# Two feed-forward layers behind an mLSTM: weights' low parts and one tile's high part of g move to GpSimd

## The chip, the cores and the metric

The kernel runs on one core of a Trainium2 chip. The metric is the device time of one launch in microseconds (us), the median of some runs. The core has five engines that run their own instruction streams in order and wait for each other through semaphores: TensorE (PE, with its weight loads as PEld), VectorE (DVE), ScalarE (ACT), GpSimd (POOL) and SyncE (SP), which here issues nearly all DMAs.

## The reference

```python
# per time step t, state C [D, D] and n [D] for each of 4 x 8 heads, D = 40, 768 steps
m_new = max(f_gate + m, i_gate)
f_stab, i_stab = exp(f_gate + m - m_new), exp(i_gate - m_new)
C = f_stab * C + i_stab * outer(v, k);  n = f_stab * n + i_stab * k
y = sigmoid(o_gate) * (C @ q) / max(abs(n . q), 1)
...
x = y, as [3072 tokens, 320]
x = relu(x @ w_in) ** 2 @ w_out            # layer 0: 320 -> 2048 -> 320
h = x @ w_in2                              # layer 1, the same sizes
out = where(h > 0, h, exp(min(h, 0)) - 1) @ w_out2
```

Everything is float32.

## The kernel before, in words

**Attention.** The recurrence is computed in chunks of 128 steps. One unit u is one chunk of one batch element (24 units), in two groups n = 2u, 2u + 1 of four heads. For a group, a row of stabilisers is loaded from DRAM, spread over 128 partitions (tile `mb`, L232), masked on GpSimd (L278), put through an exponential on ScalarE (four instructions at L286), and multiplied on VectorE with the scores from TensorE (L294, L300). `values` (L305, L310) makes a unit's outputs and state sums. VectorE adds them up (L333 to L342) and normalises (L349 to L353). GpSimd copies 64 columns of the result (L354). TensorE transposes it (L362, `in` from `xt`), and it becomes a part of the token tile x. GpSimd also multiplies the keys with a gate column (L274).

**Feed-forward.** Tokens go in six tiles of 512, and the 2048 inner columns in sixteen blocks m: 96 steps a layer. [...] A step is `mm1` (L468: eight matmuls with x's and the weights' high and low parts into the PSUM tile `h`), `elem` (the function, and the split of the result g into `hi` and `lo`), and `mm2` (L509: in layer 0 five matmuls with `hi`, then three with `lo`). In layer 0 `elem` is ReLU on ScalarE (L480), a square rounded to the high part `ghi` (L481), the same square in float32 in place (L482), and on VectorE `lo` = r - `hi` (L492). In layer 1 the high part is made by a GpSimd instruction (L491).

**Weights.** They come as 64-bit words (`raw`, L94) in 32 tiles of 704 columns, 16 a layer. ScalarE reads two fields of a word (L107, L108), VectorE puts a float32 together from them (L117, L118, L119: tile `ct`), ScalarE rounds the high part (`w_hi`, L127), and VectorE subtracts it from the whole for the low part (`w_lo`, L135). Layer 0's tiles are converted one a step, some five of them before the first step and the others during the first token tile; layer 1's during the last token tile of layer 0.

**Order.** Up to about unit 4 the order on TensorE, VectorE, ScalarE and GpSimd is that of the code. After that only TensorE's is; a scheduler places the others' instructions ahead of time, by its own estimates. TensorE writes `mm1` of step k + 1 ahead of `mm2` of step k, with a piece of attention between them in most steps. All DMAs stand in SyncE's one queue. Each engine executes its own list strictly in order.

Of the kernel before, what the change touches and what calls it, by code (L numbers as in the profile page):

```python
# [6 lines left out]
F32 = mybir.dt.float32  # L7
# [5 lines left out]
AF = mybir.ActivationFunctionType  # L13
ALU = mybir.AluOpType
# [26 lines left out]
def body(tc, qk, qp, kvo, gates, wq, ident_in, qkm_in, out):  # L41
    nc = tc.nc
    pe, act, dve, pool_, sp = nc.tensor, nc.scalar, nc.vector, nc.gpsimd, nc.sync
# [85 lines left out]
    def w_lo():  # L129
        if halves:  # L130
            i, t = halves.pop(0)
            l, f = ftiles[i]
            w = W[l, f]
            for a, k, o in [(640, 64, WC), (0, 640, WC + 64)] if l == 0 else [(0, WC, WC)]:
                dve.tensor_tensor(out=w[:, o:o + k], in0=t[:, a:a + k].bitcast(F32), in1=w[:, a:a + k].bitcast(F32), op=ALU.subtract)  # L135


    m_st = gc.tile([64, NCH + 1], F32, name="m_st")
# [333 lines left out]
    def elem(k):  # L472
        l, j, _, (c0, c1) = steps[k]
        n = c1 - c0
        h = HB.pop(k)[:, 0:n]
        r = gp.tile([128, TT], F32, tag="r", name="r")[:, 0:n]
        hi = gp.tile([128, TT], F32R, tag="ghi", name="ghi")[:, 0:n]
        lo = gp.tile([128, TT], F32R, tag="glo", name="glo")[:, 0:n]
        if l == 0:
            act.activation(out=r, in_=h, func=AF.Relu)  # L480
            act.activation(out=hi, in_=r, func=AF.Square)  # L481
            act.activation(out=r, in_=r, func=AF.Square)  # L482
        else:
            th = bp["t"].tile([128, TT], F32, tag="th", name="th")
            ex = bp["t"].tile([128, TT], F32, tag="ex", name="ex")
            act.activation(out=r, in_=h, func=AF.Relu, scale=-1.0)  # L486
            act.activation(out=th, in_=r, func=AF.Tanh, scale=0.5)  # L487
            act.activation(out=ex, in_=r, func=AF.Exp, scale=-1.0)  # L488
            dve.scalar_tensor_tensor(out=ex, in0=ex, scalar=1.0, in1=th, op0=ALU.add, op1=ALU.mult)  # L489
            dve.scalar_tensor_tensor(out=r, in0=h, scalar=0.0, in1=ex, op0=ALU.max, op1=ALU.subtract)  # L490
            pool_.tensor_scalar(out=hi, in0=r, scalar1=1.0, scalar2=1.0, op0=ALU.mult, op1=ALU.mult)  # L491
        dve.tensor_tensor(out=lo, in0=r, in1=hi.bitcast(F32), op=ALU.subtract)  # L492
        G[k] = (hi, lo)
# [174 lines left out]
    t = 2  # L668
    hs = lambda x, f: f(x) if 0 <= x < N0 else None
    us = lambda x, f: f(x // 2) if 0 <= x < N0 and x % 2 else None  # L670
    for i in range(N0 + 2):
# [19 lines left out]
        if i == N0:  # L691

            norm(B - 2)
            for f in trans(B - 2):
                f()
            x_hi(B - 2)
            idle(5)
            evac0(i - 1)
            norm(B - 1)
            x_lo(B - 2)  # L700
            for f in trans(B - 1, pacc.tile([128, 512], F32, tag="acc2", name="xt3")):
                f()
            x_hi(B - 1)
            x_lo(B - 1)
            idle(2)
            w_lo()
        if i == 0 or i > N0:
            w_begin(NF)
        if i == 2 or i > N0:
            w_lo()  # L710
# [6 lines left out]
        if i % 2 and i <= N0:  # L717
            if 1 < i < N0 - 1:
                w_lo()
            w_begin(NF)  # L720
# [24 lines left out]
    for k in range(-1, len(steps)):  # L745
        l, j, m, _ = steps[k] if k >= 0 else (0, 0, -1, None)
# [31 lines left out]
        for e in todo:  # L778
            elem(e)
# [77 lines left out]
```

## Time and profile before

| | |
|---|---|
| median of 3 runs | 869.37 us (866.83 to 874.54) |
| the profiled execution | 874.0 us, its span 870.3 us |
| granted TensorE clock, mean | 0.98 of full speed |
| TensorE matmuls busy | 824.0 us, 95% of the span |
| VectorE busy | 554.7 us, 64% |
| ScalarE busy | 540.1 us, 62% |
| GpSimd busy | 120.4 us, 14% |

The span goes from the first to the last instruction of the profiled execution. Shares over the whole span hide that the first 150 us and the rest have different limits, so the views below are by stretches. In a timeline a bracket behind an instruction says how long its engine stood idle before it and whose instruction ended that. The granted clock is TensorE's share of full speed, which falls to 0.5 in some stretches.

### The profile page before, as it was taken

What the parts mean: (1) busy time and instruction counts of PE and PEld (TensorE: products, weight loads), DVE (VectorE), ACT (ScalarE), POOL (GpSimd) and SP (SyncE); (2) the same over time, 40 slices, a digit from 0 to 9 for tenths busy, and PEclk for the clock granted to TensorE, in tenths of its full rate; (3) what the DMA queues carried; (4) which work ended last, traced back from release to release, by engine and by line L of the source; (5) the groups of instructions that cost most, each with busy time, mean ns of one, the idle gap of its engine ahead of it and who ended that gap; (6) DMA issues with size and microseconds to landing.
All of it is one profiled execution on the core that took longest, in us unless ns stands there. A gap on an engine that the chain in (4) does not pass through costs nothing.

```text
span 870.3 us, 14383 instructions
## 1 busy us (share of the span) xinstructions
PE 824.0 (95%) x5302; PEld 697.8 (80%) x5307; DVE 554.7 (64%) x994; ACT 540.1 (62%) x1035; POOL 120.4 (14%) x195
## 2 busy tenths in 40 slices
PE   9655988999999999999999998999999999999998
PEld 5544777788878878887888877999999999999997
DVE  6877995566555655645546987565565665655554
ACT  5767775665676766567558995464464554644543
POOL 3131111011111111010000002111111111111111
PEclk9978899999999999999999999999999999999999
DMA  8755563445453454445034550020020100000000
GB/s 272 227 171 180 191 197 93 134 139 141 129 143 105 128 155 119 138 129 142 2 124 142 191 171 23 1 78 1 1 79 1 49 31 2 31 1 1 31 1 31
DMA packets 32669, 85.39 MB, mean 98 GB/s; under 512 B 4087, under 2 KB 7895, under 8 KB 32599
## 3 DMA queue, kind: packets, MB, share of 16 engines
q1 hardware_dynamic: 32311, 84.15, 31.7%
q8 instruction: 41, 0.67, 0.3%
q10 hardware_dynamic: 288, 0.33, 0.1%
q14 instruction: 29, 0.24, 0.1%
HBM read 75.73 MB, written 8.73 MB: 97 GB/s over the span
## 4 chain that ended last, share of the span: by engine, by line
PE 76%; ACT 3%; DVE 3%; DMA 2%; issue 1%; POOL 1%; POOLq 0%; SPq 0%; ACTq 0%; DVEq 0%
PE h L468 35%; PE acc L509 35%; DMA mb<-negm_dr 2%; PE pv L305 1%; PE in L305 1%; PE s L294 1%; ACT mb L286 1%; PE in L362 1%; ACT ghi L481 1%; DMA kvo<-kvo 0%; DVE glo L492 0%; ACT r L480 0%; PE pv L310 0%; DVE r L490 0%; POOL mb L278 0%
## 5 line engine op out<-in xcount | busy, mean ns | idle before, releaser
L468 PE MATMUL h<-xh,w 128*128 128x512 f32 x1152 | 360.5, 394 | 0.2 <-ACT r L480 0.2
L468 PEld LDWEIGHTS h<-xh,w 128*128 128x128 f32 x1152 | 217.5, 189 | 45.3 <-ACT r L480 0.6
L492 DVE TENSOR_TENSOR glo<-r,ghi 128x512 fp32r<-128x512 f32 x192 | 133.5, 695 | 166.8 <-ACT r L482 86.1
L509 PE MATMUL acc<-w,ghi 128*128 128x320 f32 x768 | 170.3, 309 | 1.6 <-POOL ghi L491 1.6
L486 ACT ACTIVATE r<-h 128x512 f32<-128x512 f32 x96 | 57.5, 599 | 156.0 <-PE h L468 151.3
L468 PE MATMUL h<-xl,w 128*128 128x512 f32 x384 | 151.4, 394 | 0.0
L509 PEld LDWEIGHTS acc<-w,ghi 128*128 128x128 f32 x768 | 132.2, 188 | 9.8 <-POOL ghi L491 2.2
L509 PE MATMUL acc<-ghi,w 128*128 128x512 f32 x480 | 132.1, 403 | 7.3 <-ACT y L536 3.8
L509 PE MATMUL acc<-w,glo 128*128 128x320 f32 x384 | 119.1, 310 | 3.5 <-DVE glo L492 3.5
L491 POOL TENSOR_SCALAR ghi<-r 128x512 fp32r<-128x512 f32 x96 | 61.3, 638 | 361.7 <-DVE r L490 344.5
L509 PEld LDWEIGHTS acc<-ghi,w 128*128 128x128 f32 x480 | 88.2, 191 | 27.0 <-ACT y L536 6.6
L286 ACT ACTIVATE mb<-mb,cols 128x128 f32<-128x128 f32 x160 | 50.7, 389 | 81.0 <-POOL mb L278 81.0
L489 DVE SCALAR_TENSOR_TENSOR ex<-ex,th 128x512 f32<-128x512 f32 x96 | 66.5, 692 | 52.1 <-ACT ex L488 51.4
L509 PE MATMUL acc<-glo,w 128*128 128x512 f32 x288 | 84.1, 401 | 5.3 <-DVE glo L492 5.3
L468 PEld LDWEIGHTS h<-xl,w 128*128 128x128 f32 x384 | 72.8, 190 | 11.0
L480 ACT ACTIVATE r<-h 128x512 f32<-128x512 f32 x96 | 56.3, 587 | 33.7 <-PE h L468 33.1
L509 PEld LDWEIGHTS acc<-w,glo 128*128 128x128 f32 x384 | 72.1, 188 | 4.6 <-DVE glo L492 4.6
L509 PEld LDWEIGHTS acc<-glo,w 128*128 128x128 f32 x288 | 55.2, 193 | 18.8 <-DVE glo L492 6.9
L278 POOL TENSOR_SCALAR_AFFINE_SELECT mb<-mb 128x512 f32<-128x512 f32 x40 | 29.5, 748 | 281.7 <-DMA mb<-negm_dr 206.6
L481 ACT ACTIVATE ghi<-r 128x512 fp32r<-128x512 f32 x96 | 60.2, 627 | 13.3 <-PE acc L509 12.9
L490 DVE SCALAR_TENSOR_TENSOR r<-h,ex 128x512 f32<-128x512 f32 x96 | 66.3, 691 | 3.0
L487 ACT ACTIVATE th<-r 128x512 f32<-128x512 f32 x96 | 60.8, 633 | 2.7
(100 smaller groups left out, 892.3 us busy)
## 6 DMA issues: line engine op xcount, KB each, us to landing
raw<-wq SPq DMA_DIRECT2D x32, 704.0 KB, 4.3
rqk<-qk SPq DMA_DIRECT2D x32, 480.0 KB, 4.3
kvo<-kvo SPq DMA_DIRECT2D x24, 488.0 KB, 4.8
mb<-negm_dr SPq DMA_DIRECT2D x40, 256.0 KB, 4.6
qp<-qp SPq DMA_DIRECT2D x20, 256.0 KB, 4.0
y_dr<-y SPq DMA_DIRECT2D x18, 256.0 KB, 2.4
out<-y SPq DMA_DIRECT2D x22, 160.0 KB, 1.8
yr<-y_dr SPq DMA_DIRECT2D x12, 256.0 KB, 2.6
```

The source lines that it names most:

```text
L278: pool_.affine_select(out=m, in_=m, pattern=[[0, 4], [1, L]], compare_op=ALU.is_ge, fill=NEG, base=0, channel_multiplier=-1)
L286: act.activation(out=m[:, i, :], in_=m[:, i, :], func=AF.Exp, bias=cols[c % 2][:, col:col + 1])
L468: lambda i=i, a=a, b_=b_: pe.matmul(h[:, 0:n], lhsT=a, rhs=b_, start=(i == 0), stop=(i == len(seq) - 1))
L480: act.activation(out=r, in_=h, func=AF.Relu)
L481: act.activation(out=hi, in_=r, func=AF.Square)
L486: act.activation(out=r, in_=h, func=AF.Relu, scale=-1.0)
L487: act.activation(out=th, in_=r, func=AF.Tanh, scale=0.5)
L489: dve.scalar_tensor_tensor(out=ex, in0=ex, scalar=1.0, in1=th, op0=ALU.add, op1=ALU.mult)
L490: dve.scalar_tensor_tensor(out=r, in0=h, scalar=0.0, in1=ex, op0=ALU.max, op1=ALU.subtract)
L491: pool_.tensor_scalar(out=hi, in0=r, scalar1=1.0, scalar2=1.0, op0=ALU.mult, op1=ALU.mult)
L492: dve.tensor_tensor(out=lo, in0=r, in1=hi.bitcast(F32), op=ALU.subtract)
L509: ops.append(lambda: pe.matmul(o, lhsT=l_, rhs=r_, start=first and st, stop=last and sp_))
```

## The change

The low parts of all 32 weight tiles are subtracted on GpSimd and not on VectorE. In the first token tile (j = 0) of layer 0 ScalarE squares once, in float32, and GpSimd makes the high part from it, as layer 1 has it; ScalarE's other squaring falls away there. In the other tiles nothing of `elem` changes.

```diff
             for a, k, o in [(640, 64, WC), (0, 640, WC + 64)] if l == 0 else [(0, WC, WC)]:
-                dve.tensor_tensor(out=w[:, o:o + k], in0=t[:, a:a + k].bitcast(F32), in1=w[:, a:a + k].bitcast(F32), op=ALU.subtract)
+                pool_.tensor_tensor(out=w[:, o:o + k], in0=t[:, a:a + k].bitcast(F32), in1=w[:, a:a + k].bitcast(F32), op=ALU.subtract)
...
         if l == 0:
             act.activation(out=r, in_=h, func=AF.Relu)
-            act.activation(out=hi, in_=r, func=AF.Square)
-            act.activation(out=r, in_=r, func=AF.Square)
+            if j:
+                act.activation(out=hi, in_=r, func=AF.Square)
+                act.activation(out=r, in_=r, func=AF.Square)
+            else:
+                act.activation(out=r, in_=r, func=AF.Square)
+                pool_.tensor_scalar(out=hi, in0=r, scalar1=1.0, scalar2=1.0, op0=ALU.mult, op1=ALU.mult)
         else:
```

TensorE's order is the same instruction for instruction. The lists of the other engines change, since the scheduler places them anew. Behind the changed place the line numbers are 4 higher (L496 is the low part of g, L492 before); in it L485 is the float32 square and L486 the high part on GpSimd.

The first place is VectorE's list before, where unit 4's first probabilities (L300) are due, with two weight tiles ahead of them.

```order
L135 TENSOR_TENSOR w<-ct,w 128x64
L135 TENSOR_TENSOR w<-ct,w 128x640
L117 TENSOR_SCALAR ct<-ct 128x704
L118 SCALAR_TENSOR_TENSOR ct<-raw,ct 128x704
L119 ISA ct<-ct,cu 128x1408
L135 TENSOR_TENSOR w<-ct,w 128x64
L135 TENSOR_TENSOR w<-ct,w 128x640
L117 TENSOR_SCALAR ct<-ct 128x704
L118 SCALAR_TENSOR_TENSOR ct<-raw,ct 128x704
L119 ISA ct<-ct,cu 128x1408
L300 TENSOR_TENSOR mb<-s,mb 128x512
```

The same place of VectorE's list with the change:

```order
L117 TENSOR_SCALAR ct<-ct 128x704
L118 SCALAR_TENSOR_TENSOR ct<-raw,ct 128x704
L119 ISA ct<-ct,cu 128x1408
L117 TENSOR_SCALAR ct<-ct 128x704
L118 SCALAR_TENSOR_TENSOR ct<-raw,ct 128x704
L119 ISA ct<-ct,cu 128x1408
L300 TENSOR_TENSOR mb<-s,mb 128x512
```

The four L135 are gone from it; the rest keeps its order.

The second place is GpSimd's list at the first steps. Before, it holds the masks of the groups from n = 10 on (L278), the keys' multiplication (L274) and the copy into `xt` (L354).

```order
L278 AFFINE_SELECT mb<-mb 128x512 x2
L274 TENSOR_TENSOR kvo<-kvo,cols_118 128x320
L278 AFFINE_SELECT mb<-mb 128x512 x5
L354 TENSOR_SCALAR xt<-xt 128x64
L274 TENSOR_TENSOR kvo<-kvo,cols_118 128x320
```

The same place with the change; the two L486 are the high parts of g of steps 0 and 1.

```order
L278 AFFINE_SELECT mb<-mb 128x512 x2
L274 TENSOR_TENSOR kvo<-kvo,cols_118 128x320
L278 AFFINE_SELECT mb<-mb 128x512 x3
L135 TENSOR_TENSOR w<-ct,w 128x64
L135 TENSOR_TENSOR w<-ct,w 128x640
L486 TENSOR_SCALAR ghi<-r 128x512
L135 TENSOR_TENSOR w<-ct,w 128x64
L135 TENSOR_TENSOR w<-ct,w 128x640
L278 AFFINE_SELECT mb<-mb 128x512 x2
L486 TENSOR_SCALAR ghi<-r 128x512
L354 TENSOR_SCALAR xt<-xt 128x64
```

Step 0's high part stands behind the masks up to n = 14, step 1's behind those of n = 15 and 16, and a pair of low parts stands ahead of each.

The third place is ScalarE's list at step 11 of the first token tile, behind the exponentials of group 19. Before:

```order
L286 ACTIVATE mb<-mb,cols_117 128x128 x4
L480 ACTIVATE r<-h 128x512
L481 ACTIVATE ghi<-r 128x512
L482 ACTIVATE r<-r 128x512
L480 ACTIVATE r<-h 128x512
```

With the change:

```order
L286 ACTIVATE mb<-mb,cols_117 128x128 x4
L480 ACTIVATE r<-h 128x512
L108 ACTIVATE cu<-raw 128x704
L485 ACTIVATE r<-r 128x512
L480 ACTIVATE r<-h 128x512
```

One of the two squares is gone, and a piece of a weight tile's conversion (L108) has come between ReLU and square.

## Rows read from the trace of the kernel before

**Rows 1.** Table of windows: each engine's busy us (instructions), clock, DMA share, GB/s

```profile
core 0: us, PE busy (x) PEld busy (x) DVE busy (x) ACT busy (x) POOL busy (x), PEclk, DMA share, GB/s
...
43.00:70.00 27.00, 14.25 (x50) 10.02 (x51) 17.48 (x30) 19.11 (x49) 8.61 (x11) 0.75 0.50 164
70.00:92.50 22.50, 15.89 (x116) 12.96 (x116) 20.53 (x39) 15.46 (x27) 3.84 (x4) 0.73 0.62 203
92.50:131.00 38.50, 34.82 (x280) 27.97 (x278) 35.06 (x72) 30.35 (x54) 4.01 (x6) 1.00 0.61 185
...
150.00:500.00 350.00, 345.95 (x2404) 284.79 (x2403) 208.99 (x422) 235.17 (x458) 28.68 (x54) 1.00 0.44 128
```

**Rows 2.** Timeline of TensorE: start, duration in us, instructions, idle time before and releaser

```profile
58.43 2.07 PE L294 MATMUL s<-rqk 120*128 120x128 f32 x8 [7.91 <-DVE mb L300]
...
63.36 1.42 PE L509 MATMUL acc<-ghi,w 128*128 128x512 f32 x5 [0.43 <-ACT ghi L481]
68.59 1.65 PE L509 MATMUL acc<-glo,w 128*128 128x512 f32 x3 [3.81 <-DVE glo L492]
70.17 1.39 PE L305 MATMUL in<-cf,qp 104*64 104x84 f32 x16
...
74.90 1.31 PE L509 MATMUL acc<-ghi,w 128*128 128x512 f32 x5
...
85.86 0.66 PE L362 MATMUL in<-ident,xt 128*128 128x128 f32 x2 [6.25 <-DVE xt L353]
...
89.09 2.48 PE L509 MATMUL acc<-ghi,w 128*128 128x512 f32 x5
...
143.33 2.30 PE L509 MATMUL acc<-ghi,w 128*128 128x512 f32 x5 [3.00 <-ACT ghi L481]
```

**Rows 3.** Groups of VectorE, 92.5 to 131 us: busy us, mean ns, idle before

```profile
L119 DVE CUSTOM_DVE_ANT_0 ct<-ct,cu 128x1408 uint16<-128x1408 uint16 x7 | 6.2, 887 | 0.8 <-ACT cu L108 0.7
L118 DVE SCALAR_TENSOR_TENSOR ct<-raw,ct 128x704 int32<-128x704 int32 x6 | 5.7, 957 | 0.0
L135 DVE TENSOR_TENSOR w<-ct,w 128x640 fp32r<-128x640 f32 x6 | 4.9, 816 | 0.0
L492 DVE TENSOR_TENSOR glo<-r,ghi 128x512 fp32r<-128x512 f32 x7 | 4.8, 685 | 0.3 <-ACT r L482 0.3
```

**Rows 4.** Groups of GpSimd over the whole span, the same columns

```profile
L491 POOL TENSOR_SCALAR ghi<-r 128x512 fp32r<-128x512 f32 x96 | 61.3, 638 | 361.7 <-DVE r L490 344.5 <-PE h L468 9.1 <-PE acc L509 8.2
...
L274 POOL TENSOR_TENSOR kvo<-kvo,cols 128x320 f32<-128x320 f32 x20 | 15.7, 784 | 41.7 <-DMA kvo<-kvo 32.1 <-ACT qks L252 4.0 <-ACT mb L286 2.3
```

**Rows 5.** Timelines of VectorE and GpSimd at two places, near 31 and near 103 us

```profile
31.25 0.69 DVE L300 TENSOR_TENSOR mb<-s,mb 128x512 f32<-128x512 f32 x1
...
31.40 0.72 POOL L274 TENSOR_TENSOR kvo<-kvo,cols 128x320 f32<-128x320 f32 x1
...
102.88 0.82 DVE L135 TENSOR_TENSOR w<-ct,w 128x640 fp32r<-128x640 f32 x1
...
103.26 0.93 POOL L278 TENSOR_SCALAR_AFFINE_SELECT mb<-mb 128x512 f32<-128x512 f32 x1 [11.38 <-DVE den L349]
...
103.61 1.32 DVE L118 SCALAR_TENSOR_TENSOR ct<-raw,ct 128x704 int32<-128x704 int32 x1
```

**Rows 6.** Timelines of GpSimd (first row) and VectorE, 42 to 59 us

```profile
42.49 0.63 POOL L278 TENSOR_SCALAR_AFFINE_SELECT mb<-mb 128x512 f32<-128x512 f32 x1 [10.37 <-DMA mb<-negm_dr]
...
47.80 0.95 DVE L135 TENSOR_TENSOR w<-ct,w 128x64 fp32r<-128x64 f32 x2
...
53.05 1.59 DVE L135 TENSOR_TENSOR w<-ct,w 128x64 fp32r<-128x64 f32 x2 [0.86 <-ACT w L127]
...
57.69 0.68 DVE L300 TENSOR_TENSOR mb<-s,mb 128x512 f32<-128x512 f32 x1
```

**Rows 7.** Timelines of SyncE's DMA issues and of GpSimd, 71 to 82 us

```profile
72.54 0.84 SPq L232 DMA_DIRECT2D mb<-negm_dr  x2
...
78.83 2.22 POOL L278 TENSOR_SCALAR_AFFINE_SELECT mb<-mb 128x512 f32<-128x512 f32 x2 [22.82 <-DMA mb<-negm_dr]
```

**Rows 8.** Groups of ScalarE, 92.5 to 131 us: busy us, mean ns, idle before

```profile
L108 ACT ACTIVATE cu<-raw 128x704 int32<-128x704 uint32 x7 | 5.9, 841 | 0.0
...
L482 ACT ACTIVATE r<-r 128x512 f32<-128x512 f32 x6 | 3.8, 627 | 0.1
```

## The prediction

> **What bounds the kernel now.** I first read the table of busy time by stretches. From 150 us on TensorE is busy 345.95 of 350 us at a granted clock of 1.00 [rows 1]: no work that leaves VectorE or ScalarE there can shorten anything. The slack is ahead of 150 us, in the first token tile, where attention, the conversion of sixteen weight tiles and the first feed-forward steps share the engines: TensorE is busy 14.25 of 27.0, 15.89 of 22.5 and 34.82 of 38.5 us, the first two at a clock of about 0.74 [rows 1]. The second reading is TensorE's timeline with its waits [rows 2]: 7.91 us for VectorE's L300 (probabilities), 3.81 us for the low part of g, 6.25 us for VectorE's L353 (normalised attention output), 3.00 us for ScalarE's high part. [...] The third is VectorE by groups between 92.5 and 131 us: 35.06 of 38.5 us busy [rows 1], half of it weight conversion (L119 6.2, L118 5.7, and six low-part pairs) [rows 3]. So in the first tile VectorE is nearly full while GpSimd has 4 to 9 us of work in each stretch [rows 1]. That is the room that the change uses.
>
> **Prices on GpSimd.** A weight's low part on VectorE is a pair, 64 and 640 columns, 0.95 us together [rows 6]. GpSimd's nearest row with two inputs is L274, 320 columns: 0.72 us alone, 0.784 in the mean [rows 4, 5]. With one input 512 columns cost 0.638 [rows 4]. For 640 columns the one-input rate gives 0.80, twice L274 gives 1.57; I take 1.3, since it is the same operation as L274 and part of L274's time is fixed. With 0.25 for the 64-column piece (a fifth of L274 and a start of 0.1) a pair costs 1.55 us (bounds 1.05 to 1.9). The high part of g is the instruction of L491: 0.64 us [rows 4].
>
> [...]
>
> **The two engines shut each other out.** At 102.88 VectorE's low part runs 0.82 us; GpSimd's mask starts at 103.26 and takes 0.93 us; VectorE's L118 then starts at 103.61 and takes 1.32 us, where its mean is 0.957 [rows 3, 5]. The mask's own time is 0.63 [rows 6]: it stood until the low part was over, and L118 stood until the mask was over. Where VectorE reads PSUM (L300 at 31.25, 0.69 us, as long as at 57.69) L274 ran beside it in 0.72 us [rows 5, 6]. So a GpSimd microsecond is not free: it stops VectorE unless VectorE then works from PSUM or idles.
>
> **Term 1, the opening (43 to 70 us).** VectorE runs from 47.80 to 58.37 before L300 is out, with two low parts in it: 0.95, and 0.86 of waiting plus 1.59 [rows 6]. Both go, 3.4 us. GpSimd does the first pair while VectorE waits anyway; the second holds the next conversion for 1.3 us. L300 is 2.1 us earlier. The high part of step 0 now waits in GpSimd's queue behind masks, multiplications and a pair: TensorE gets it some 1 us later than at 63.36. But ScalarE no longer writes it, and the square is no longer behind eleven exponentials, so the 3.81 us for the low part shrink under 1. The attention matmuls of 70.17 [rows 2] come 2 us earlier. Bounds: 0 (the gain lost to the masks) to -4. **-2.**
>
> **Term 2 (70 to 92.5 us).** GpSimd's order now has the masks of two score groups ahead of step 1's high part. Their data are issued at 72.54 and land when the masks start, 78.83 [rows 7], 8.66 us after the attention matmuls start at 70.17 [rows 2], because buffers are freed by these very matmuls. Two masks at 0.63 and the high part at 0.64 end 10.6 us after them. Step 1's second half starts there now 4.73 us after (74.90) [rows 2]: a new wait of 5.9 us. Behind it the wait of 6.25 us for L353 is gone, as VectorE does the normalisation during the new one. To the transposes it is 10.6, then 4.7 us of work (74.90 to 79.6, 85.86 less 6.25), plus 1.7 for the lower clock: 17.0, against 15.7 now. But what follows the transposes runs at the full clock and not at half: 3 us less (2.48 to 1.31 is one part of it [rows 2]). **-1.5**; bounds -4 (data land sooner) to +2 (both stretches at half clock).
>
> **Term 3 (92.5 to 131 us).** VectorE is 35.06 of 38.5 busy [rows 1]. Six pairs go: 35.06 - 5.7 = 29.4. GpSimd gets six pairs and seven high parts: 6 x 1.55 + 7 x 0.64 = 13.8 us, of which about a tenth is start and end: 12.4. How much of that stops VectorE? L119, L118 and L492 alone, all with both inputs in SBUF, are 16.7 of the 29.4 [rows 3], 0.56; with the other such operations I take 0.8, so 9.9. Half of the 3.4 us of idle time stays (ScalarE has seven squarings less). 29.4 + 9.9 + 1.7 = 41.0: VectorE becomes the bound and the stretch is 2.5 us longer. Bounds: TensorE's own 34.82, -3.7; pairs at 1.9 and all of it in VectorE's way, +8. **+2.5.**
>
> **Term 4 (step 11).** TensorE's wait that ends at 143.33 [rows 2] hangs on a mask, four exponentials, ReLU and high part. In ScalarE's new order a weight conversion stands between ReLU and square, and the GpSimd pass comes behind: 0.84 [rows 8] and 0.64. **+1.5** (0 to +2).
>
> **At nothing:** the first 43 us, where VectorE gets lighter but the transposes hang on a mask whose data land at 42.49 [rows 6] whatever VectorE does, and the second layer's sixteen low parts, which run under a full TensorE [rows 1] with GpSimd otherwise empty. Without that cover each would cost what it holds VectorE up, about 1.4 us.
>
> **Sum.** -2 - 1.5 + 2.5 + 1.5 = +0.5 us. The profiled execution took 874.0 us (span 870.3), at the top of the three runs shown (866.83 to 874.54, median 869.37). It becomes 874.5; on the median that is **870 us**.
>
> **Rivals.** *Faster.* GpSimd works mostly where VectorE waits or reads PSUM. Then term 3 falls to TensorE's own 34.82 us, -3.7, term 2 to -4, term 1 to -4 and term 4 to 0: -11.7, 858 us. For it: nearly all the idle time of TensorE sits in these stretches. Against it: VectorE is 91% busy in the third [rows 1], and every GpSimd row that met a conversion was stretched [rows 5, 6]. Chance of over 1%: 0.17.
>
> *Slower: the high part comes late at every step.* Between the end of a step's first half and the start of its second TensorE has two blocks of eight matmuls, 2.1 us each at 0.26 a matmul (1.31 for five, 74.90) [rows 2], 4.2 us. The new chain is ReLU and square, 0.6 each [rows 8], then GpSimd: 0.4 for VectorE's lock, a pair of 1.55 that stands ahead, 0.4 again, and 0.64: 4.2 us. This decides: any delay more, a conversion ahead on ScalarE (0.84) [rows 8] or data on which a GpSimd instruction ahead waits, stops TensorE at every step, 0.8 us at thirteen steps, 10 us, and the clock falls with it: 881 us. For it: one queue now carries masks that wait for DMAs (22.82 us once [rows 7]) and the high part. Against it: attention matmuls lie between in half of the steps. Chance of over 1%: 0.21. [...]
>
> *About the same,* the sum above, its own range 865 to 877: 0.62.
>
> A change of 1% (8.7 us) is about what a measurement of this kernel can tell from none: faster 0.17, same 0.62, slower 0.21. The range reaches into both rivals: 860 to 881.
>
> **What would show it.** Right: L135 on GpSimd at 1.3 us or more for 640 columns; TensorE waiting 5 to 6 us for GpSimd's L486 once near 75 us, and no wait for L353 behind it; L118 and L119 stretched beyond 1.2 us at many places; TensorE's busy share from 92.5 us to the end of the sixteenth step under 0.9. Wrong: pairs beside VectorE's conversions with neither stretched (then the faster rival), or TensorE waiting for L486 at most steps (the slower one).

## The result, and the profile after

The changed kernel takes 879.23 us in the median (877.11 to 879.98), the kernel before 868.26 us beside it (866.83 to 874.54). The ratio is 1.011 with a 95% interval of 1.0073 to 1.0146: about 9.6 us slower. The profiled execution of the changed kernel took 879.98 us, its span 878.2 us.

First the table of windows of the changed kernel, for the stretches of [rows 1] and two more (start and end in us, length, then busy us and instructions of each engine, granted clock, DMA share, GB/s):

```profile
core 0: us, PE busy (x) PEld busy (x) DVE busy (x) ACT busy (x) POOL busy (x), PEclk, DMA share, GB/s
0.00:43.00 43.00, 38.83 (x302) 26.44 (x302) 28.89 (x60) 26.43 (x72) 16.61 (x28) 0.86 0.81 255
43.00:70.00 27.00, 17.45 (x101) 12.83 (x100) 19.84 (x34) 18.91 (x47) 17.10 (x19) 0.69 0.47 158
70.00:92.50 22.50, 18.10 (x129) 14.74 (x129) 17.45 (x29) 13.57 (x27) 9.62 (x13) 0.81 0.52 169
92.50:131.00 38.50, 33.46 (x262) 26.59 (x261) 34.21 (x55) 27.05 (x48) 24.06 (x25) 0.94 0.67 205
...
485.00:520.00 35.00, 30.62 (x125) 23.01 (x126) 33.61 (x35) 31.19 (x49) 13.96 (x8) 1.00 0.48 165
```

The same view of the kernel before, for the two stretches that no table of it has shown so far:

```profile
0.00:43.00 43.00, 35.18 (x348) 23.91 (x352) 31.14 (x78) 28.49 (x75) 12.08 (x22) 0.98 0.79 251
485.00:520.00 35.00, 35.00 (x156) 29.00 (x155) 32.12 (x45) 34.20 (x57) 0.52 (x1) 1.00 0.55 178
```

Up to 92.5 us the changed kernel gets through 532 matmuls and the kernel before through 514: a little more work in the same time, as forecast, although it is 46 matmuls behind at 43 us, where the granted clock is 0.86 against 0.98. The surprise is the last row. From 485 to 520 us TensorE was busy all the time before (35.00 of 35.00); now it is busy 30.62 us, at the full clock. There it waits for VectorE. The waits of TensorE over the whole span of the changed kernel (who waits for whom: us in total, times, longest):

```profile
PE acc L513 <- POOL ghi L486: 10.4, 4, 4.4
PE acc L513 <- DVE glo L496: 8.9, 12, 2.3
PE s L294 <- DVE mb L300: 6.3, 1, 6.3
PE in L362 <- DVE xt L353: 4.4, 3, 1.9
```

The second line is the surprise: eleven of the twelve waits, 8.8 us of the 8.9, lie between 420 and 545 us. TensorE's timeline shows the large waits of the first token tile, and two of the eleven (start, duration in us, instructions, idle time before and releaser):

```profile
30.59 0.94 PE L305 MATMUL pv<-kvo,mb 128*64 128x42 f32 x16 [1.95 <-DVE num L622]
...
60.54 2.07 PE L294 MATMUL s<-rqk 120*128 120x128 f32 x8 [6.32 <-DVE mb L300]
67.84 2.11 PE L513 MATMUL acc<-ghi,w 128*128 128x512 f32 x5 [2.26 <-POOL ghi L486]
...
79.90 2.50 PE L513 MATMUL acc<-ghi,w 128*128 128x512 f32 x5 [4.40 <-POOL ghi L486]
...
146.25 2.02 PE L513 MATMUL acc<-ghi,w 128*128 128x512 f32 x5 [3.22 <-POOL ghi L486]
...
499.13 0.96 PE L513 MATMUL acc<-glo,w 128*128 128x512 f32 x3 [0.51 <-DVE glo L496]
...
503.58 0.98 PE L513 MATMUL acc<-glo,w 128*128 128x512 f32 x3 [0.54 <-DVE glo L496]
```

Two steps of the last stretch lie 503.58 - 499.13 = 4.45 us apart. What VectorE does in that time is its timeline of the changed kernel:

```profile
498.38 0.69 DVE L496 TENSOR_TENSOR glo<-r,ghi 128x512 fp32r<-128x512 f32 x1
498.99 0.52 DVE L117 TENSOR_SCALAR ct<-ct 128x704 int32<-128x704 int32 x1
499.55 2.35 DVE L118 SCALAR_TENSOR_TENSOR ct<-raw,ct 128x704 int32<-128x704 int32 x1
502.03 0.89 DVE L119 CUSTOM_DVE_ANT_0 ct<-ct,cu 128x1408 uint16<-128x1408 uint16 x1
502.84 0.69 DVE L496 TENSOR_TENSOR glo<-r,ghi 128x512 fp32r<-128x512 f32 x1
```

and the same loop in the kernel before, three rows of VectorE's timeline and two of TensorE's:

```profile
496.28 0.89 DVE L118 SCALAR_TENSOR_TENSOR ct<-raw,ct 128x704 int32<-128x704 int32 x1
497.09 0.88 DVE L135 TENSOR_TENSOR w<-ct,w 128x704 fp32r<-128x704 f32 x1
...
500.11 0.89 DVE L118 SCALAR_TENSOR_TENSOR ct<-raw,ct 128x704 int32<-128x704 int32 x1
...
485.42 0.84 PE L509 MATMUL acc<-glo,w 128*128 128x512 f32 x3
...
489.05 0.84 PE L509 MATMUL acc<-glo,w 128*128 128x512 f32 x3
```

L135 (0.88 us) has left VectorE, but L118 next to it has grown from 0.89 to 2.35 us. GpSimd's timeline of the changed kernel, at this place and at two at which TensorE waited for L486, shows why:

```profile
59.09 1.87 POOL L278 TENSOR_SCALAR_AFFINE_SELECT mb<-mb 128x512 f32<-128x512 f32 x2
...
61.88 2.58 POOL L278 TENSOR_SCALAR_AFFINE_SELECT mb<-mb 128x512 f32<-128x512 f32 x3
64.43 2.76 POOL L135 TENSOR_TENSOR w<-ct,w 128x64 fp32r<-128x64 f32 x2
67.17 0.61 POOL L486 TENSOR_SCALAR ghi<-r 128x512 fp32r<-128x512 f32 x1
...
77.52 1.47 POOL L278 TENSOR_SCALAR_AFFINE_SELECT mb<-mb 128x512 f32<-128x512 f32 x2 [7.31 <-DMA mb<-negm_dr]
78.97 0.88 POOL L486 TENSOR_SCALAR ghi<-r 128x512 fp32r<-128x512 f32 x1
...
499.43 1.72 POOL L135 TENSOR_TENSOR w<-ct,w 128x704 fp32r<-128x704 f32 x1 [2.74 <-ACT w L127]
```

The low part starts at 499.43, 0.12 us ahead of L118's 499.55, and ends at 501.15. L118 ends at 501.90, 0.75 us later. It stood until the other instruction was over, and then ran about its own time. VectorE's step became 502.84 - 498.38 = 4.46 us, longer than the 3.63 us of a step in which TensorE doesn't wait (489.05 - 485.42 in the kernel before). VectorE had no room there before either: from one L118 to the next it took 500.11 - 496.28 = 3.83 us, a little more than TensorE's step, and TensorE waited for `glo` only at the end of the stretch (3.3 us in three waits, 523 to 534 us).

### The profile page after: what moved, and what is told of

It is laid out like the page before. It is cut to its first block, busy times and chain, and to the rows that moved or that the text cites. A ratio compares the mean times of both kernels' runs of the same rounds, so it can differ in the third digit from the quotient of the medians.

```text
span 878.2 us, 14388 instructions
## 1 busy us (share of the span) xinstructions
PE 835.2 (95%) x5307; PEld 703.7 (80%) x5307; DVE 566.4 (64%) x946; ACT 533.6 (61%) x1019; POOL 194.8 (22%) x259
## 4 chain that ended last, share of the span: by engine, by line
PE 76%; DVE 10%; issue 4%; POOL 4%; ACT 3%; DMA 2%; POOLq 0%; DVEq 0%; ACTq 0%
PE acc L513 34%; PE h L468 33%; DVE ct L118 3%; DMA mb<-negm_dr 2%; PE pv L305 2%; POOL w L135 2%; DVE ct L119 2%; PE s L294 2%; PE in L305 2%; DVE ct L117 1%; DVE glo L496 1%; PE dps L634 1%; POOL mb L278 1%; PE in L362 1%; ACT w L127 1%
## 5 line engine op out<-in xcount | busy, mean ns | idle before, releaser
L496 DVE TENSOR_TENSOR glo<-r,ghi 128x512 fp32r<-128x512 f32 x192 | 138.9, 723 | 159.7 <-POOL ghi L495 75.1
L513 PEld LDWEIGHTS acc<-w,ghi 128*128 128x128 f32 x768 | 132.2, 188 | 10.2 <-POOL ghi L495 2.9
L135 POOL TENSOR_TENSOR w<-ct,w 128x64 fp32r<-128x64 f32 (+2 forms) x48 | 65.9, 1387 | 76.5 <-ACT w L127 76.3
L278 POOL TENSOR_SCALAR_AFFINE_SELECT mb<-mb 128x512 f32<-128x512 f32 x40 | 28.2, 710 | 222.1 <-DMA mb<-negm_dr 162.8
```

The source lines that it names most:

```text
L135: pool_.tensor_tensor(out=w[:, o:o + k], in0=t[:, a:a + k].bitcast(F32), in1=w[:, a:a + k].bitcast(F32), op=ALU.subtract)
L278: pool_.affine_select(out=m, in_=m, pattern=[[0, 4], [1, L]], compare_op=ALU.is_ge, fill=NEG, base=0, channel_multiplier=-1)
L513: ops.append(lambda: pe.matmul(o, lhsT=l_, rhs=r_, start=first and st, stop=last and sp_))
```

## The experiments

Runs were measured in three groups (1 to 4, 5 to 8, 9 to 12), each beside the kernel before, whose medians were 868.62, 871.78 and 867.65 us. Each ratio is to the kernel before of its group, with a 95% interval. Between groups a ratio can move by more than its interval: runs 5 and 11 are the same kernel and came out at 0.9952 and 1.0024.

| | where the low parts run, layer 0 / layer 1 | high part, first tile | median us | ratio (interval) |
|---|---|---|---|---|
| changed kernel | GpSimd / GpSimd | GpSimd | 879.23 | 1.011 (1.0073 to 1.0146) |
| 1 | GpSimd / VectorE | GpSimd | 868.67 | 1.0004 (0.9973 to 1.0034) |
| 2 | VectorE / GpSimd | ScalarE | 875.61 | 1.0088 (1.0056 to 1.0119) |
| 3 | GpSimd / VectorE | ScalarE | 860.52 | 0.9902 (0.9864 to 0.9939) |
| 4 | VectorE / VectorE | GpSimd | 869.36 | 1.0014 (0.9983 to 1.0046) |
| 5 | GpSimd from the fourth tile / VectorE | ScalarE | 867.36 | 0.9952 (0.9921 to 0.9984) |
| 6 | GpSimd / VectorE | GpSimd, not at steps 0, 1, 11 | 867.49 | 0.995 (0.9917 to 0.9983) |
| 7 | VectorE / left out, zeros | ScalarE | 865.04 | 0.9942 (0.9905 to 0.9979) |
| 8 | as 7, and a free subtraction | ScalarE | 871.87 | 1.0012 (0.9974 to 1.0049) |
| 9 | as 7, and a subtraction once a step | ScalarE | 877.86 | 1.0111 (1.0071 to 1.0151) |
| 10 | as 3 | ScalarE | 861.21 | 0.9918 (0.9887 to 0.995) |
| 11 | as 5 | ScalarE | 869.84 | 1.0024 (0.9997 to 1.0051) |
| 12 | as 2, in four pieces | ScalarE | 877.47 | 1.0104 (1.0067 to 1.014) |

### Runs 1 and 2: which layer's low parts cost

Run 1 is the changed kernel with one word more; run 2 is the kernel before with the opposite choice.

```diff
 # run 1, from the changed kernel
-                pool_.tensor_tensor(out=w[:, o:o + k], ...
+                (pool_ if l == 0 else dve).tensor_tensor(out=w[:, o:o + k], ...
 # run 2, from the kernel before
-                dve.tensor_tensor(out=w[:, o:o + k], ...
+                (dve if l == 0 else pool_).tensor_tensor(out=w[:, o:o + k], ...
```

> The changed kernel, with the second layer's sixteen low parts back on VectorE; the first layer's low parts and the high part of g in the first token tile stay on GpSimd. Theory (the whole loss comes in the last token tile of layer 0, where GpSimd's 1.72 us low part stops VectorE once a step; the first-layer edits cancel to about zero): the +10.2 us at 528 us goes, 867 to 871 us, ratio to the kernel before 1.000 (0.996 to 1.004), and no wait for the low part of g between 485 and 533 us. Rival 1 (GpSimd's late high part is the loss): stays at 877 to 880. Rival 2 (every GpSimd low part costs the same by shutting VectorE out, in both layers): half of the loss goes, 873 to 875.

> The kernel before, with only the second layer's sixteen low parts on GpSimd. Theory: +8 to +9 us, 876 to 878 (ratio 1.009 to 1.011), with L135 at 1.7 us or more and VectorE's loop at about 4.4 us a step from 485 to 533 us. Rival 1 (late high part): 868, ratio 1.000. Rival 2 (each low part the same): +4 to +5, 873.

Run 1 came out at 1.0004 and run 2 at 1.0088, 7.6 us. Both are what the theory said, within half a us, and neither rival gives them. One sign of run 1 failed: two waits for the low part of g are left near the end (3.3 us), as the kernel before has them. The second layer's sixteen low parts cost 8 to 10 us, whether the rest of the change is there (1.011 against 1.0004) or not.

The traces give this cost with less noise. Up to some 436 us or later, runs 2, 7, 8, 9 and 12 have the instruction lists of the kernel before, and run 1 those of the changed kernel. One L509, which starts at 395.22 in the kernel before, serves as a mark in all of them. From it to the end of the span the profiled executions take:

| second layer's low parts | from the mark to the end, us |
|---|---|
| on VectorE (kernel before; runs 1, 3, 4, 5, 6, 10, 11) | 475.1; 474.9 to 475.4 |
| on GpSimd (changed kernel; run 2) | 484.0; 483.9 |
| on GpSimd in four pieces (run 12) | 483.9 |
| zeros (run 7) | 472.0 |
| zeros and the subtractions of runs 8 and 9 | 476.9 and 485.2 |

So the second layer's low parts on GpSimd cost 8.9 us, alone and in company. VectorE's L118 in run 2, from its groups of 485 to 520 us (busy us, mean ns, idle before), is stretched as in the changed kernel:

```profile
L118 DVE SCALAR_TENSOR_TENSOR ct<-raw,ct 128x704 int32<-128x704 int32 x8 | 17.3, 2162 | 0.3
```

In the kernel before L118 takes 0.89 us in the same stretch; eight of them lose 8 x 1.27 = 10.2 us, where the eight L135 that left VectorE had taken 7.1.

### Runs 3 and 4: the first layer's low parts and the high part of g, each alone

```diff
 # run 3, from the kernel before; run 4 is the changed kernel with dve in this line
-                dve.tensor_tensor(out=w[:, o:o + k], ...
+                (pool_ if l == 0 else dve).tensor_tensor(out=w[:, o:o + k], ...
```

> The kernel before, with only the first layer's sixteen pairs of low parts on GpSimd; ScalarE still makes the high part of g, VectorE the second layer's low parts. Theory: the early loss (+4 us at 47 us) and the earlier L300 (-2) as in the changed kernel, no wait for a GpSimd high part at steps 0, 1 and 11 (so without their 2.3, 4.4 and 3.2 us), VectorE still shut out from 92 to 131 us (+2): 866 to 871, ratio 0.997 to 1.003. Rival 1 (late high part is the loss): 866 or less, below 0.998. Rival 2: +4 to +5, 873.

> The changed kernel, with all low parts back on VectorE: only the high part of g in the first token tile is made by GpSimd. Theory: nothing changes ahead of 58 us; a late high part at the first steps and step 11 (some us), the wait for the low part at 68.59 gone, ScalarE lighter: 865 to 870, ratio 0.996 to 1.002. Together with the run that has only the first layer's low parts on GpSimd it should add up to the run with both. Rival 1: 875 to 880, with waits for L486 at most steps. Rival 2: 868.

Run 3 is 1% faster than the kernel before, 0.9902. The theory had no such gain (0.997 at best), rival 1 had it as "below 0.998"; for run 4 rival 1 fails, with 1.0014 where it wanted 875 us or more. Run 4 is at 1.0014. If the two edits added up, both together would be 0.9916; run 1, which has both, is at 1.0004. So they don't add up: the high part on GpSimd costs nothing while the weights' low parts stay on VectorE, and about 8 us (868.67 against 860.52) when they are on GpSimd too. The waits of TensorE from 43 to 150 us point to where. First run 3:

```profile
PE s L294 <- DVE mb L300: 6.6, 1, 6.6
PE acc L509 <- DVE glo L492: 6.0, 4, 2.3
...
PE in L362 <- POOL xt L354: 2.9, 2, 2.6
```

and run 1:

```profile
PE acc L513 <- POOL ghi L486: 9.8, 4, 3.9
PE s L294 <- DVE mb L300: 6.5, 1, 6.5
```

GpSimd's late high part is the largest wait of run 1, and run 3 has more waits for VectorE in its place; in sum all waits are 22 us in run 1 and 20 in run 3. But the clock differs too. Table of windows, run 3:

```profile
70.00:92.50 22.50, 18.54 (x154) 14.61 (x148) 20.61 (x35) 18.17 (x35) 13.51 (x12) 1.00 0.67 217
```

and run 1:

```profile
70.00:92.50 22.50, 18.58 (x132) 15.06 (x132) 18.64 (x30) 13.77 (x27) 10.76 (x13) 0.83 0.52 169
```

From 70 to 92.5 us TensorE is busy for the same time, but run 1 gets through 132 matmuls and run 3 through 154. Behind the waits for GpSimd at steps 1 and 11 TensorE runs at a lower clock (0.87 against 1.00 from 131 to 150 us, too); run 3 has neither wait. By the traces the price of the high part on GpSimd is thus the waits and the clock behind them; run 6 was to show it. Rival 1 of the first runs, a late high part, would then be no rival but a second cause, inside the first layer, and there it is hidden by the gain of the other edit. Freeing VectorE of the first layer's low parts is by itself worth 1%, and the high part takes all of it back.

### Run 6: is it the three long waits?

```diff
 # from run 1
-            if j:
+            if j or m in (0, 1, 11):
                 act.activation(out=hi, in_=r, func=AF.Square)
```

> The changed kernel with the second layer's low parts on VectorE (868.67), and with ScalarE making the high part of g at steps 0, 1 and 11, the three at which TensorE waited for GpSimd. GpSimd still makes it at the other thirteen steps. Theory (the high part on GpSimd costs 8 us beside the low parts, and these three waits of 2.3, 4.4 and 3.2 us are where): 860 to 863, ratio 0.990 to 0.994. Rival (the high part costs by shutting VectorE out at every step, and the waits hide others that come instead): 865 to 868, ratio 0.996 to 1.000.

The ratio, 0.995, lies between the ranges of the two expectations (run 1 has 1.0004, run 3 0.9902). By the ratios about half of the price goes; but the runs are of two groups, the medians differ by 1.2 us only (867.49 against 868.67), and the intervals of runs 1 and 6 overlap. TensorE's waits from 43 to 150 us in this run:

```profile
PE acc L513 <- DVE glo L496: 7.6, 3, 4.5
...
PE acc L513 <- POOL ghi L486: 3.6, 3, 2.1
```

GpSimd's waits fall from 9.8 to 3.6 us, and a wait of 4.5 us for VectorE's low part comes in the place of step 1's, since the scheduler placed VectorE's list anew. So whether the three long waits are the price of the high part isn't settled: taking them away brought others.

### Runs 5, 10 and 11: the first 43 us

The changed kernel loses 4 us in the opening: the transpose that started at 43.39 (by its weight load) starts at 47.35. The same transpose starts between 41.7 and 43.4 us in the nine profiled executions with the early pairs on VectorE, and between 46.6 and 47.5 in the five with them on GpSimd. Rows of the changed kernel's timelines of GpSimd, VectorE and TensorE show how the loss begins:

```profile
24.58 1.82 POOL L135 TENSOR_TENSOR w<-ct,w 128x64 fp32r<-128x64 f32 x2
...
25.05 1.74 DVE L117 TENSOR_SCALAR ct<-ct 128x704 int32<-128x704 int32 x1
26.82 1.29 DVE L118 SCALAR_TENSOR_TENSOR ct<-raw,ct 128x704 int32<-128x704 int32 x1
...
34.26 2.01 PE L595 MATMUL acc<-rqk 40*128 40x128 f32 x8
```

The pair on GpSimd holds L117 (0.53 us alone) for 1.2 us, the keys' multiplication (L274) holds L118 for 0.4, and TensorE waits 1.95 us at 30.59. Behind that wait the matmuls run at half clock (0.50 granted from 32 to 48 us; 1.00 in the kernel before from 30 to 38): L595 takes 2.01 us for eight, where the kernel before takes 1.10 (L591 there). How much of the 4 us is the clock isn't settled: over the first 43 us it is 0.79 to 0.86 in the five executions, but 0.87 to 1.00 in the nine, and of these the one at 0.87 (run 5) has its transpose at 42.29, no later than most. Run 5 keeps the three early pairs on VectorE; 10 and 11 are runs 3 and 5 once more, side by side.

```diff
 # from run 3
-                (pool_ if l == 0 else dve).tensor_tensor(...
+                (pool_ if l == 0 and f >= 3 else dve).tensor_tensor(...
```

> The kernel before, with the first layer's low parts on GpSimd from the fourth tile on: the three pairs that are due before 43 us stay on VectorE. Theory (pairs on GpSimd between 24 and 34 us stop VectorE's conversion and by it TensorE, 2 us, and the half clock that follows makes 6 of it, of which 3 to 4 are left at 47 us): TensorE's transposes of 43.39 stand where they stood, clock 0.95 or more over the first 43 us, all the gains behind stay: 856 to 859, ratio 0.985 to 0.990. Rival (the early loss is swallowed by waits that follow, so taking it away frees nothing): 860 to 862, ratio 0.990, as with all pairs of the first layer on GpSimd.

> The kernel before with the first layer's sixteen pairs on GpSimd once more, beside the one that keeps three early pairs on VectorE, on one chip. Theory (the gain of 1% is the opening and the stretch up to 100 us, and it is the program's): ratio 0.987 to 0.993 again. Rival (the other chip's runs flattered it): 0.995 to 1.000.

> The kernel that keeps the three early pairs on VectorE, on the same chip as the one without. Theory (the scheduler's other order between 85 and 124 us loses more than the early stretch gives back): 3 to 5 us slower than its neighbour, ratio to before 0.994 to 0.998. Rival (chips differ): equal to its neighbour within 0.2%.

Run 5 came out at 0.9952, slower than run 3, so the first expectation failed, and its rival too. Side by side the difference is larger, and larger than run 11's own expectation: 0.9918 against 1.0024. Run 10 bears out run 3. The early loss itself goes with the pairs: the same transpose's weight load starts at 42.65 in run 11 and at 47.40 in run 10 (the clock over the first 43 us is 0.98 and 0.79). But with three pairs fewer on GpSimd the scheduler gives VectorE another list, in which a conversion stands ahead of the low part of g. GpSimd's and VectorE's timeline of run 11 and what TensorE waits for:

```profile
85.53 2.47 POOL L135 TENSOR_TENSOR w<-ct,w 128x64 fp32r<-128x64 f32 x2 [1.66 <-ACT w L127]
...
86.74 2.00 DVE L119 CUSTOM_DVE_ANT_0 ct<-ct,cu 128x1408 uint16<-128x1408 uint16 x1
88.67 0.68 DVE L492 TENSOR_TENSOR glo<-r,ghi 128x512 fp32r<-128x512 f32 x1
...
89.40 1.65 PE L509 MATMUL acc<-glo,w 128*128 128x512 f32 x3 [2.98 <-DVE glo L492]
```

L119 is held for 1.1 us by a pair on GpSimd, and `glo` stands behind it. TensorE waits 12.5 us for `glo` in run 11 between 20 and 150 us (six times), 4.5 us in run 10. So 4.7 us ahead at 43 us become 4.3 us behind at a transpose of 146 us (145.94 against 141.67 in run 10). With an order planned ahead, an edit of one stretch moves the others; what the early pairs cost by themselves was seen, not got back.

### Runs 7, 8, 9 and 12: does GpSimd shut VectorE out, or is its result late?

Runs 7 to 9 leave out the second layer's low parts (zeros stand there), so that nothing waits for a subtraction.

```diff
 # run 7, from the kernel before
+            if l == 1:
+                pool_.memset(w[:, WC:2 * WC].bitcast(F32), 0.0)
 # run 8: and on a scratch tile of its own
+                pool_.tensor_tensor(out=scr, in0=scr, in1=scr, op=ALU.subtract)
 # run 9: the same, reading the tile's high part
+                pool_.tensor_tensor(out=scr, in0=scr, in1=w[:, 0:WC], op=ALU.subtract)
 # runs 7 to 9
+                return
```

> The kernel before, with the second layer's low parts left out: GpSimd writes zeros in their place (0.52 us for 512 columns in the opening, so about 0.7 for 704; no input is read), VectorE doesn't subtract. Theory (the loss of 7.6 us with the second layer's low parts on GpSimd is time in which a two-input GpSimd instruction keeps VectorE from starting): VectorE's loop is 3.0 us of its own and less than TensorE's 3.63, so 866 to 869, ratio 0.998 to 1.000. Rival (any GpSimd instruction on the way from the high part to the weights costs it, by its semaphores and its place in the chain): 872 to 876.

> As the run with zeros for the second layer's low parts (which are left out), plus a GpSimd subtraction of 704 columns per tile on a scratch buffer in SBUF, whose result no instruction waits for. Theory (shutting out): the loss is back although nothing waits for it: 874 to 878, ratio 1.006 to 1.011, with L118 or L119 of VectorE stretched from 0.89 to 2 us or more. Rival (the chain over GpSimd costs, not the shutting out): as with the zeros alone, within 1 us.

> The kernel with zeros for the second layer's low parts (which are left out), plus per tile one GpSimd subtraction of 704 columns that reads the tile's high part, so that it comes once a step where the low part came, and writes a scratch buffer that no other engine reads. Theory (shutting out, once a step): VectorE's own 3.0 us a step and 1.4 held make 4.4, above TensorE's 3.63, although nothing waits for the result: between 485 and 533 us TensorE loses 7 us or more against the kernel with zeros alone (ratio 0.994 to before), so 1.001 to 1.006 of before; TensorE waits for VectorE's L495 most of the steps. Rival (the way over GpSimd costs by its result): the stretch as with zeros alone, ratio 0.994 (0.991 to 0.998).

Run 7, at 0.9942, is faster than expected. Its trace says why: from the mark to the end it takes 3.1 us less than the kernel before, so VectorE's subtractions held TensorE up even there. Run 8 is at 1.0012, but it doesn't test what it should: the free subtractions have no inputs to wait for, and fourteen of the sixteen ran in bunches between 437 and 471 us, nine of them in one stretch of 14.84 us. Run 9 ties each to its tile, and is at 1.0111, above its range: about 15 us over run 7 by the ratios of two groups, and 13.3 us by the traces from the mark to the end (485.2 against 472.0), although nothing but GpSimd itself reads what is computed. Its timelines of GpSimd, VectorE and TensorE:

```profile
495.58 2.34 POOL L136 TENSOR_TENSOR scr<-scr,w 128x704 f32<-128x704 f32 x1 [2.36 <-ACT w L127]
...
496.26 2.22 DVE L496 TENSOR_TENSOR glo<-r,ghi 128x512 fp32r<-128x512 f32 x1
...
498.53 0.96 PE L513 MATMUL acc<-glo,w 128*128 128x512 f32 x3 [0.61 <-DVE glo L496]
```

`glo` takes 2.22 us for 0.69 and TensorE waits for it. So the shutting out by itself is enough for the loss; the rival, that the way over GpSimd costs by its result, falls. TensorE and ScalarE wait for none of these GpSimd instructions there. Run 9 has a memset of 0.69 us a step more on GpSimd than the changed kernel, so its size isn't comparable one to one.

Run 12 cuts the low part into pieces.

```diff
 # from run 2
-  ... else [(0, WC, WC)]:
+  ... else [(i * WC // 4, WC // 4, WC + i * WC // 4) for i in range(4)]:
```

> The kernel before with the second layer's low parts on GpSimd, each cut into four instructions of 176 columns. Theory A (GpSimd's whole time counts, however it is cut): as in one piece, ratio 1.008 to 1.012, VectorE's loop 4.4 us or more. Theory B (only one long hold counts; VectorE slips in between pieces and loses 0.4 us at most each time it meets one): ratio 1.000 to 1.004, and no wait for the low part of g in most of the steps.

The time, 1.0104, is that of theory A, but its sign is missing. GpSimd and VectorE by groups, 485 to 520 us:

```profile
L135 POOL TENSOR_TENSOR w<-ct,w 128x176 fp32r<-128x176 f32 x29 | 23.1, 829 | 9.9 <-ACT w L127 6.6 <-PE h L468 3.3
...
L118 DVE SCALAR_TENSOR_TENSOR ct<-raw,ct 128x704 int32<-128x704 int32 x7 | 7.3, 1044 | 0.1
L117 DVE TENSOR_SCALAR ct<-ct 128x704 int32<-128x704 int32 x8 | 5.0, 626 | 7.8 <-ACT ct L107 7.8
```

VectorE's L118 is stretched by 0.15 us only, as theory B has it. Now GpSimd stands instead: a piece takes 0.83 us in the mean (0.55 at the least), and four of them 3.3 us against 1.72 in one. GpSimd gives up the converted tile that much later, ScalarE waits for it before the next tile's first field (L107, 7.2 us for L135 over the run), and VectorE idles 7.8 us for L107. Smaller pieces turned the wait round, and the loss stayed (483.9 us from the mark, as in one piece). So run 12 bears out neither theory as it was put: the whole time counts, but on the other engine.

## Why the prediction was right or wrong

The time fell into the range, near its upper end, but the likeliest case was "about the same", and the kernel is 1.1% slower. The interval of the ratio begins at 0.73%, so slower by over 1% is likely but not certain. That the range held is luck: its upper end came from the rival on the slow side, which is not what happened, and the loss came from a term put at nothing. The signs named in advance came all in all (a wait of 4.40 us for L486, none for L353 behind it, L118 and L119 stretched, TensorE busy 33.46 of 38.5 us), but they concern the first layer alone and could not show this.

**At nothing, the second layer: the step that failed.** The prediction put its sixteen low parts at nothing, "under a full TensorE". It named their price without that cover, 1.4 us each, and never looked at whether VectorE had the room. A full TensorE is cover only while VectorE keeps up with it. The trace of the kernel before would have told it: VectorE is 32.12 of 35 us busy in that stretch, at 3.83 us a step against TensorE's 3.63. With one low part off (0.88) and the prediction's own 1.4 on, that is 4.35. With the change one low part is off and a hold of 1.46 on: 0.69 + 0.52 + 2.35 + 0.89 = 4.45 against 3.63, 0.82 a step over the eleven steps in which TensorE waited, 9 us. Runs 1, 2 and 9 show it: 7.6 us by run 2's ratio, 8.9 by the traces. The sentence that no work that leaves VectorE or ScalarE behind 150 us can shorten anything is wrong too: the subtractions left out in run 7 were worth 3.1 us. The row that it rests on ends at 500 us, and TensorE's three waits for `glo` lie at 523 to 534.

**At nothing, the first 43 us: wrong by 4 us in the trace.** "VectorE gets lighter" overlooked that a pair on GpSimd holds the next conversion by 1.2 us where the pair had cost VectorE 0.95, and that TensorE ran at half clock (0.50) behind the wait of 1.95 us. The wait behind the mask that was to cover it (3.57 us before, for GpSimd's L354) took up only a part.

**Price of a pair: 1.55 taken, 1.82 measured** where it wasn't held (24.58: 0.32 for the 64 columns, 1.54 for the 640), and 1.72 for 704 columns. An estimate from the first two: 2.1 ns a column and 0.19 us that is fixed. That is 1.92 times VectorE's 0.95 for the pair and 1.95 times its 0.88 for the 704. The bound of 1.9 held. The prediction took 1.3 for the 640 columns, between its two rates; what was measured is close to twice L274, 1.57.

**The two engines shut each other out: right**, and the core of the result. L135 starts at 499.43 and L118 at 499.55, and L118 ends 0.75 us behind L135, its own time being 0.89. The prediction weighed this in the first layer (terms 1 and 3) and not in the second.

**Term 1, the opening: -2, the trace gives -3** (from 4.0 us behind at 47.35 to 1.0 behind at the attention matmuls, 71.16 against 70.17). L300 makes up 1.9 us, the low part's wait is gone (5.3 us of waits for L492 ahead of 420 us before, none here), and the high part costs TensorE 2.26 us at 67.84, behind five masks and a pair, where 1 was forecast.

**Term 2: -1.5, the trace gives -3.4** (1.0 behind becomes 2.4 ahead: 90.17 against 92.54). **The rows were right, the reason wrong.** The new wait of 5.9 us came as 4.40 at 79.90, for the data of two masks. The wait of 6.25 us for L353 is gone. But the prediction held that VectorE catches up during the new wait, so that one pays for the other. Run 3 has no such wait, and its transposes start at 78.31 without one for L353 (one of them waits 2.65 us for GpSimd's L354): VectorE was in time because the low parts had left it. By this the new wait bought nothing, which would explain why the high part costs 8 us in company and nothing alone: in run 4 a wait of 3.96 us for L486 stands where the kernel before waits 6.25 for L353. The term's own numbers add up to -1.7, not -1.5. Its 1.7 us for the lower clock and its 3 us for the full clock behind the transposes were estimates. From the second half of step 1 to the transposes the changed kernel takes 7.2 us (79.90 to 87.12, granted clock 0.50 from 80 to 84), where the kernel before has 4.7 of work; from the transposes to the end of the stretch it takes 3.05 us (87.12 to 90.17) against 6.68 (85.86 to 92.54), at 1.00 from 86 to 92 us against 0.50.

**Term 3: +2.5, the trace gives +3.2** (127.96 against 127.15 at the next transposes). VectorE is 34.21 of 38.5 us busy and TensorE 33.46 at 0.94 of the clock. VectorE's L119 takes 1.26 us in the mean there (0.887 before [rows 3]), the 640-column low part on GpSimd 1.88 (1.54 at 24.58): both engines hold each other.

**Term 4: +1.5, the trace gives +2.1** (146.25 against 143.33). The wait of step 11 is 3.22 us, at 146.25, and the five matmuls behind it take 2.02 us, as they took 2.30 behind the wait of before [rows 2].

These are differences of two profiled executions, and executions that run the same lists differ: the kernel before and run 2 by 5.5 us at the mark (395.22 and 389.73). So each stretch is read from six executions with the lists of before and from two with the changed lists (changed kernel and run 1). A stretch ends at the instruction that has this start in the kernel before:

| stretch ends at | forecast | lists of before, us | changed lists, us | difference of medians |
|---|---|---|---|---|
| 43.39 | nothing | 41.7 to 43.4 | 47.5, 47.2 | +4.5 |
| 70.17 (term 1) | -2 | 25.9 to 26.8 | 23.7, 23.9 | -2.5 |
| 92.54 (term 2) | -1.5 | 20.8 to 22.9 | 19.0, 18.4 | -3.6 |
| 127.15 (term 3) | +2.5 | 34.6 to 35.2 | 37.8, 37.8 | +3.1 |
| 143.33 (term 4) | +1.5 | 14.9 to 16.2 | 18.3, 18.1 | +2.7 |
| 395.22 | nothing | 247.9 to 251.9 | 248.0, 247.8 | -1.1 |

The signs of all four terms are borne out, and the sum up to the mark is +3.1 us, with some us of noise. Run 1's ratio of 1.0004, with an interval that reaches to +3 us, gives it as about nothing, against +0.5 us forecast. **Its size was about right; its two edits were not seen apart.** That one of them is a gain of 1% and the other a loss of the same size only runs 3 and 4 show.

**The slower rival: not so.** TensorE waited for L486 four times, not at thirteen steps. At the other twelve steps of the tile the matmuls in between were cover enough. The fall of the clock that its 881 us count in was an estimate; measured are 2.11, 2.50 and 2.02 us for the five matmuls behind the waits of 2.26, 4.40 and 3.22 us, and 1.39 at 88.26, where no wait stands ahead.

The version that beats both kernels is run 3: only the first layer's low parts on GpSimd, 860.52 and 861.21 us in two measurements, 0.9902 and 0.9918 of the kernel before.

## What to carry to other kernels

A neighbour that is full covers nothing by itself: TensorE, busy 35.00 of 35 us before, was busy 30.62 of them once VectorE was held. Before putting an edit at nothing, add up the step of the engine that the edit holds, with the hold in it, and compare it with the step of the bounding engine. The low part moved from VectorE to GpSimd was paid twice, by its longer time (1.72 us for 0.88 on 704 columns) and by the VectorE instruction that stood while it ran (L118, 2.35 us for 0.89). It gained between 43 and 92 us, where TensorE stood waiting for VectorE's attention work, and lost where it held weight conversions that were due: in the first 43 us, from 92 to 131 us, and in the last token tile of layer 0. Edits of one change that share a queue are measured one by one and together: here one alone gave 1%, and the other took it back only in its company.

## What was unexpected of the hardware

A one-input VectorE instruction from SBUF was held as well: L117 took 1.74 us for 0.53 while a pair ran on GpSimd. And cutting the two-input GpSimd instruction in four didn't make it yield at less cost: 176 columns took 0.83 us in the mean beside a busy VectorE, 704 took 1.72 when it began first.
